# Grouped-query attention on one core: a new order of the PV matmuls, of the early loads, and of the work at the end

## The chip, the cores and the metric

One core of one Trainium2 chip. The time is the device time of one execution in microseconds (us). Times of experiments are compared with runs of the kernel before on the same chip in the same rounds. "Span" is the profiled execution from its first to its last instruction, some 1.7 us less than the device time.

## The reference, cut to what matters

```python
B, Hq, Hkv, Sq, Sk, D = 16, 32, 8, 288, 512, 128      # bf16
def reference(q, k, v):
    k = jnp.repeat(k, 4, axis=1); v = jnp.repeat(v, 4, axis=1)
    scores = jnp.einsum("bhqd,bhkd->bhqk", q, k) * D ** -0.5
    return jnp.einsum("bhqk,bhkd->bhqd", softmax(scores), v)
```

Four query heads share one key/value head, so there are 128 heads of 4 x 288 = 1152 queries (9 query tiles of 128) and 512 keys (4 key tiles of 128).

## The kernel before

Each head is cut into three chunks of 1536 score columns, 384 chunks in all. For a chunk TensorE makes the scores (S, keys on the partitions), ScalarE the exponentials, and TensorE the product with the values (PV): three query tiles, each a sum over four key tiles. A column of ones behind the 128 value columns makes the sum of the exponentials, hence 129 columns. VectorE inverts that sum and scales. Keys and values come in units of four heads, queries by head. All loads and stores are issued by the sync engine, in one fixed order. The code is abridged (`...` marks what is left out; the wrappers around the calls are dropped).

```python
    DV = D + 1                # 129
    LAG = NC + 1              # PV runs 4 chunks behind S
    NQ = 12                   # query buffers, one head each
    NO = 6                    # output buffers, one head each
    ALONE = 5 * TPC           # sums that the last check takes by themselves
    ...
        v_sb = sbuf_tensor("v_sb", [P, NSLOT, UG * NJ, DV], BF16)   # rows of 129, packed
    ...
        def op_pv(r):                      # 12 matmuls of one chunk
            waits = [("s_vc", g + 1), ("s_e", ...)]
            if 2 <= r < NS - 1:
                waits.append(("s_ev", r - 1))
            for a in range(TPC):           # query tile
                for j in range(NJ):        # key tile
                    matmul(outs(r)[:, a, :], pt_sb[..j, t..], v_sb[:, sl, gi * NJ + j, :],
                           start=(j == 0), stop=(j == NJ - 1))

        def op_ev(r):                      # VectorE: scale into an output buffer
            waits = [("s_rc", r + 1)]
            if g >= NO:                    # the buffer's last store must have landed
                waits.insert(0, ("s_o%d" % (g % NO), 16 * (g // NO)))

        # the sync engine's order: a list sorted by a time in chunks
        for u in range(1, NU):             # keys and values by unit
            t = -1.0 + u if u < NSLOT else NC * UG * (u - NSLOT + 1) + LAG
            sp.append((t, op_k(u))); sp.append((t + 0.2, op_v(u)))
        for g in range(UG, NG):            # queries by head
            sp.append((-0.9 + g / UG - 1.0 if g < NQ else NC * (g - NQ + 1) + 1.2, op_q(g)))
        for g in range(LASTG):             # output by head
            sp.append((NC * (g + 1) + LAG + 1.5, op_store(g)))
```

A kernel for any data ("general code") is built in as well. At the end a flag, made from the extremes of the sums, tells each engine whether to run it; with these inputs none does.

Of the kernel before, what the change touches and what calls it, by code (L numbers as in the profile page):

```python
# [287 lines left out]
def bass_standalone__gqa_softmax__near_ridge_kernel(  # L288
# [6 lines left out]
    B, Hq, Sq, D = q.shape  # L295
# [3 lines left out]
    NJ = Sk // P  # L299
    NT = R // P  # L300
    G = Hkv
    NG = B * G
    assert D == P and Sk % P == 0 and R % P == 0
    BANK = 512
    TPC = 3
    CH = TPC * BANK
    COLS = NJ * R
    NC = COLS // CH
# [3 lines left out]
    LAG = NC + 1  # L312
    UG = 4
    NU = NG // UG
    NSLOT = 3
    NQ = 12
    NPT = 3
    NO = 6
    NS = NG * NC
    LASTG = NG - 1  # L320
    ALONE = 5 * TPC


    q_v = q.rearrange("b h s d -> (b h s) d").rearrange("(x t) d -> x (t d)", t=NT)
# [4 lines left out]
    with ExitStack() as es:  # L329
# [29 lines left out]
        def general(eng, key, after):  # L359

            home[key] = nc.cur_bb
            eng.br(after + key)
            with nc.body("general_" + key):
                if key == "sp":
                    eng.sem_inc(sem["s_go"], 1)
                fns[key](eng)
                eng.br("done_" + key)
            nc.switch_bb(after + key)
# [20 lines left out]
        v_sb = main.enter_context(nc.sbuf_tensor("v_sb", [P, NSLOT, UG * NJ, DV], BF16))  # L389
# [4 lines left out]
        rl_sb = main.enter_context(nc.sbuf_tensor("rl_sb", [P, NG * NT], FP32))  # L394
        st_sb = main.enter_context(nc.sbuf_tensor("st_sb", [P, 2, B], FP32))
        ck_sb = main.enter_context(nc.sbuf_tensor("ck_sb", [P, 3], FP32))
        bad_sb = main.enter_context(nc.sbuf_tensor("bad_sb", [P, 2, ALONE + 1], FP32))
        one_f = main.enter_context(nc.sbuf_tensor("one_f", [P, 1], FP32))
# [6 lines left out]
        def need(eng, waits):  # L405

            left = []
            for (s, n) in waits:
                key = (id(eng), s)
                if seen.get(key, 0) < n:  # L410
                    seen[key] = n
                    left.append((sem[s], n))
            return left

        def emit(eng, waits, fn):
            waits = need(eng, waits)
            for (s, n) in waits[:-1]:
                eng.wait_ge(s, n)
            ins = fn()
            if waits:  # L420
                ins.wait_op(waits[-1][0], waits[-1][1], "sem-ge")
            return ins


        def op_k(u, gi=None):
            eng = nc.sync
            sl = u % NSLOT
            if u >= NSLOT:
                for (s, n) in need(eng, [("s_s", NC * UG * (u - NSLOT + 1))]):
                    eng.wait_ge(s, n)  # L430
            g0, g1 = (0, UG) if gi is None else (gi, gi + 1)
            eng.dma_start_transpose(  # L432
                kt_sb[:, sl, :, g0:g1].rearrange("d j g p -> d j (g p)"),
                k_v[(u * UG + g0) * P:(u * UG + g1) * P]
            ).then_inc(sem["us_k%d" % sl if gi is None else "s_k%d" % gi], 16)

        def op_v(u, gi=None):
            eng = nc.sync
            sl = u % NSLOT
            if u >= NSLOT:  # L440
                for (s, n) in need(eng, [("s_vc", UG * (u - NSLOT + 1))]):
                    eng.wait_ge(s, n)
            g0, g1 = (0, UG) if gi is None else (gi, gi + 1)
            eng.dma_start(
                vd_sb[:, sl, g0:g1], v_v[:, u * UG + g0:u * UG + g1]
            ).then_inc(sem["us_v%d" % sl if gi is None else "s_v%d" % gi], 16)

        def op_q(g):
            eng = nc.sync
            if g >= NQ:  # L450
                for (s, n) in need(eng, [("s_s", NC * (g - NQ + 1))]):
                    eng.wait_ge(s, n)
            eng.dma_start_transpose(qt_sb[:, g % NQ], q_v[g * P:(g + 1) * P]).then_inc(sem["s_q%d" % (g % NQ)], 16)
# [49 lines left out]
        def outs(r):  # L503

            if r == NS - 1:
                return ps_s[:, (NS - 2) % 2].rearrange("p (a e) -> p a e", e=BANK)[:, :, 0:DV]
            return ps_o[:, r % 2, 0:TPC * DV].rearrange("p (a e) -> p a e", e=DV)

        def op_pv(r):
            eng = nc.tensor  # L510
            g = r // NC
            sl, gi = (g // UG) % NSLOT, g % UG
            waits = [("s_vc", g + 1), ("s_e", r + 1 if g == LASTG else NC * (g + 1))]
            if 2 <= r < NS - 1:
                waits.append(("s_ev", r - 1))
            for a in range(TPC):
                t = TPC * (r % NC) + a
                for j in range(NJ):
                    ins = emit(eng, waits if a == 0 and j == 0 else [], lambda: eng.matmul(  # L519
                        outs(r)[:, a, :], pt_sb[:, g % NPT, j * R + t * P:j * R + (t + 1) * P],  # L520
                        v_sb[:, sl, gi * NJ + j, :], start=(j == 0), stop=(j == NJ - 1)))
            ins.then_inc(sem["s_pv"], 1)


# [53 lines left out]
        def op_stat(b):  # L578
            eng = nc.vector
            w = G * NT  # L580
            a, e = b * w, (b + 1) * w - (ALONE if b == B - 1 else 0)
            emit(eng, [("s_rc", e // TPC)], lambda: eng.tensor_reduce(  # L582
                st_sb[:, 0, b:b + 1], rl_sb[:, a:e], AX.X, ALU.max))
            eng.tensor_reduce(st_sb[:, 1, b:b + 1], rl_sb[:, a:e], AX.X, ALU.min).then_inc(sem["s_stat"], 1)  # L584

        def op_over(hi, lo, x0, x1, wait, n):

            eng = nc.vector
            emit(eng, [wait], lambda: eng.tensor_scalar(  # L589
                out=bad_sb[:, 0, x0:x1], in0=hi, scalar1=SUM_MAX, scalar2=None, op0=ALU.is_gt)  # L590
            ).then_inc(sem["s_stat"], 1)
            emit(eng, [("s_stat", n)], lambda: eng.scalar_tensor_tensor(  # L592
                out=bad_sb[:, 1, x0:x1], in0=lo, scalar=1.0 / SUM_MAX, in1=bad_sb[:, 0, x0:x1],
                op0=ALU.is_lt, op1=ALU.add)).then_inc(sem["s_bad"], 1)
# [2 lines left out]
        first = [lambda: op_k(0, 0), lambda: op_q(0), lambda: op_k(0, 1), lambda: op_q(1), lambda: op_v(0, 0)]  # L597
        first += [lambda: op_k(0, 2), lambda: op_q(2), lambda: op_v(0, 1)]
        first += [lambda: op_k(0, 3), lambda: op_q(3), lambda: op_v(0, 2), lambda: op_v(0, 3)]
        sp = []  # L600
        for u in range(1, NU):
            t = -1.0 + u if u < NSLOT else NC * UG * (u - NSLOT + 1) + LAG
            sp.append((t, lambda u=u: op_k(u)))
            sp.append((t + 0.2, lambda u=u: op_v(u)))
        for g in range(UG, NG):
            sp.append((-0.9 + g / UG - 1.0 if g < NQ else NC * (g - NQ + 1) + 1.2, lambda g=g: op_q(g)))
        for g in range(LASTG):
            sp.append((NC * (g + 1) + LAG + 1.5, lambda g=g: op_store(g)))
        for i in range(NC):
# [13 lines left out]
        def _(eng):  # L623
            for n in range(NS + LAG):
# [6 lines left out]
            emit(eng, [("s_ev", NS - 1), ("s_bad", 2)], lambda: eng.matmul(  # L631
                ps_o[0:1, NS % 2, 0:ALONE + 1], one_f[:], bad_sb[:, 1, :], start=True, stop=True)
            ).then_inc(sem["s_bad"], 1)
            choose(eng, "pe", behind=True)

        @block.scalar
        def _(eng):
            emit(eng, [("s_one", 1)], lambda: eng.activation(dum[:, 1:2], dum[:, 0:1], ACTF.Exp))  # L638
            for n in range(NS):
                op_exp(n)  # L640
            op_ev_last()
            general(eng, "act", "end_")
            choose(eng, "act")

        @block.gpsimd
# [7 lines left out]
        @block.vector  # L653
        def _(eng):
            eng.memset(dum[:], 0.0).then_inc(sem["s_one"], 1)  # L655
            eng.memset(one_f[:], 1.0)
            general(eng, "dve", "main_")
            per_b = G * NC
            for r in range(NS):
                op_rc(r)  # L660
                if r == NS - 1:
                    last = rl_sb[:, NG * NT - ALONE:NG * NT]
                    op_over(last, last, 0, ALONE, ("s_rc", NS), B + 3)
                op_ev(r)
                if r % per_b == per_b - 1 and r < NS - 1:
                    op_stat(r // per_b)
                if r == NS - 1 - ALONE // TPC:
                    op_stat(B - 1)
                    emit(eng, [("s_stat", B)], lambda: eng.tensor_reduce(  # L669
                        ck_sb[:, 0:1], st_sb[:, 0, :], AX.X, ALU.max))  # L670
                    eng.tensor_reduce(ck_sb[:, 1:2], st_sb[:, 1, :], AX.X, ALU.min).then_inc(sem["s_stat"], 1)  # L671
                    op_over(ck_sb[:, 0:1], ck_sb[:, 1:2], ALONE, ALONE + 1, ("s_stat", B + 1), B + 2)
            with nc.allow_low_precision(reason="a count of at most 2048"):
                emit(eng, [("s_bad", 3)], lambda: eng.tensor_reduce(  # L674
                    flag_i[:], ps_o[0:1, NS % 2, 0:ALONE + 1], AX.X, ALU.add)).then_inc(sem["s_flag"], 1)
            choose(eng, "dve")
# [30 lines left out]
```

## Time and profile before

| | before |
|---|---|
| time, median of 3 runs | 540.84 us (540.35 to 541.56) |
| span, mean TensorE clock | 539.4 us, 0.996 |
| first exponential starts | 8.18 us |
| last exponential ends | 533.16 us |
| from there to the end | 6.22 us |

Names in the lines of the profile: PE is TensorE and PEld its weight loads, ACT is ScalarE, DVE is VectorE, SPq is the sync engine issuing a load or store. `kt_sb`, `qt_sb` and `vd_sb` are the buffers into which keys, queries and values are loaded, `v_sb` the values as PV reads them, `ps_s` the scores, `pt_sb` their exponentials, `ps_o` the PV sums, `o_sb` the output buffers. L541 is line 541 of the kernel.

Two engines are busy 97% of the span, TensorE and ScalarE. From the page, the busy tenths in 40 slices of the span and the clock that TensorE was granted:

```profile
PE   4799999999999999999999999999999999999997
...
ACT  5889999999999999999999999999999999999995
...
PEclk9989999999999999999999999999999999999999
```

Only the first three slices (13.5 us each) and the last one have room in them. The single 8 of the clock row is a time at half clock, at 27 to 30 us, after the one stall.

### The profile page before, as it was taken

How to read it: one execution, taken by the hardware profiler on the slowest of the kernel's cores; microseconds unless marked ns; L12 is line 12 of the kernel's file. 1: busy time of each engine (PE TensorE's matmuls, PEld its weight loads, DVE VectorE, ACT ScalarE, POOL GpSimd, SP SyncE). 2: the span in 40 equal slices, each digit the busy share in tenths (PEclk: the TensorE clock that was granted, in tenths of full speed). 3: DMA queues.
4: the chain of work that ended last, by engine and by line, in shares of the span. 5: the costliest groups of instructions: out<-in, count | busy, mean ns of one | idle time of the engine just before them, and what ended most of it. 6: DMA issues, size and time to landing. Idle time of an engine off the chain costs nothing.

```text
span 539.4 us, 14538 instructions
## 1 busy us (share of the span) xinstructions
PE 524.0 (97%) x6152; PEld 411.2 (76%) x6152; DVE 288.5 (53%) x809; ACT 522.1 (97%) x387; POOL 73.8 (14%) x133
## 2 busy tenths in 40 slices
PE   4799999999999999999999999999999999999997
PEld 1577777777777777777777777777777777777776
DVE  0445555555555555555555555555555555555555
ACT  5889999999999999999999999999999999999995
POOL 1021211100111101111101111101111101111000
PEclk9989999999999999999999999999999999999999
DMA  6999999999899988899998999989899988995212
GB/s 133 178 216 246 281 247 292 260 203 190 219 212 228 207 209 219 192 215 232 205 183 220 219 215 233 211 186 199 224 220 225 219 182 216 204 224 154 87 67 92
DMA packets 253944, 110.08 MB, mean 204 GB/s; under 512 B 220848, under 2 KB 237616, under 8 KB 253872
## 3 DMA queue, kind: packets, MB, share of 16 engines
q1 hardware_dynamic: 253872, 109.08, 90.2%
q8 instruction: 50, 0.82, 0.6%
q14 instruction: 22, 0.18, 0.1%
HBM read 16.78 MB, written 37.75 MB: 101 GB/s over the span
## 4 chain that ended last, share of the span: by engine, by line
PE 94%; ACT 3%; DVE 1%; DMA 1%; issue 1%; SPq 0%
PE ps_o L519 49%; PE ps_s L499 45%; ACT pt_sb L537 3%; DMA qt_sb<-in_q_dram 1%; DVE o_sb L565 0%; SPq L432 0%; DVE rl_sb L554 0%; DVE bad_sb L589 0%; DVE bad_sb L592 0%; DVE ck_sb L669 0%; DVE st_sb L584 0%; DVE flag_i L674 0%; DVE st_sb L582 0%; DVE ck_sb L671 0%
## 5 line engine op out<-in xcount | busy, mean ns | idle before, releaser
L537 ACT ACTIVATE pt_sb<-ps_s 128x1536 bf16<-128x1536 f32 x384 | 520.2, 1452 | 10.6 <-PE ps_s L499 10.6
L519 PEld LDWEIGHTS ps_o<-v_sb,pt_sb 128*128 128x128 bf16 x4596 | 300.2, 98 | 55.0 <-DVE o_sb L565 0.6
L519 PE MATMUL ps_o<-v_sb,pt_sb 128*128 128x129 bf16 x4596 | 332.6, 221 | 0.4 <-DVE o_sb L565 0.4
L499 PE MATMUL ps_s<-qt_sb,kt_sb 128*128 128x512 bf16 (+3 forms) x1542 | 313.8, 326 | 11.6 <-DMA qt_sb<-in_q_dram 6.7
L565 DVE TENSOR_TENSOR o_sb<-ps_o,rl_sb 128x384 bf16<-128x384 f32 x383 | 213.6, 558 | 13.5 <-DVE rl_sb L554 0.3
L554 DVE RECIPROCAL rl_sb<-ps_o 128x3 f32<-128x3 f32 x383 | 69.3, 181 | 233.9 <-PE ps_o L519 233.9
L499 PEld LDWEIGHTS ps_s<-qt_sb,kt_sb 128*128 128x128 bf16 x1542 | 130.2, 98 | 69.5 <-DMA qt_sb<-in_q_dram 6.7
L547 POOL COPY v_sb<-vd_sb 128x512 bf16<-128x512 bf16 x128 | 73.3, 616 | 421.3 <-DMA vd_sb<-in_v_dram 392.5
L584 DVE TENSOR_REDUCE st_sb<-rl_sb 128x1 f32<-128x72 f32 (+1 forms) x16 | 3.5, 217 | 0.0
L582 DVE TENSOR_REDUCE st_sb<-rl_sb 128x1 f32<-128x72 f32 (+1 forms) x16 | 3.5, 217 | 0.0
L573 ACT ACTIVATE o_sb<-ps_s,rl_sb 128x128 bf16<-128x128 f32 x1 | 0.4, 368 | 2.9 <-DVE rl_sb L554 2.9
L638 ACT ACT_TABLE_LOAD x1 | 1.3, 1283 | 0.8 <-PEq L692 0.8
L631 PE MATMUL ps_o<-bad_sb,one_f 128*1 128x16 f32 x2 | 0.2, 176 | 0.7 <-DVE bad_sb L592 0.7
L519 PE MATMUL ps_s<-v_sb,pt_sb 128*128 128x129 bf16 x12 | 0.9, 221 | 0.0
L631 PEld LDWEIGHTS ps_o<-bad_sb,one_f 128*1 128x1 f32 x2 | 0.1, 80 | 0.9 <-DVE bad_sb L592 0.9
L519 PEld LDWEIGHTS ps_s<-v_sb,pt_sb 128*128 128x128 bf16 x12 | 0.7, 98 | 0.0
L655 DVE MEMSET dum<- 128x2 f32 x1 | 0.1, 60 | 0.9 <-PEq L692 0.9
L565 DVE TENSOR_TENSOR o_sb<-ps_s,rl_sb 128x256 bf16<-128x256 f32 x1 | 0.4, 418 | 0.0
L647 POOL MEMSET v_sb<- 128x48 bf16 x1 | 0.3, 311 | 0.3 <-POOLq L692 0.3
L638 ACT ACTIVATE dum<-dum 128x1 f32<-128x1 f32 x1 | 0.2, 203 | 0.0
L592 DVE SCALAR_TENSOR_TENSOR bad_sb<-rl_sb,bad_sb 128x15 f32<-128x15 f32 x1 | 0.2, 175 | 0.0
L589 DVE TENSOR_SCALAR bad_sb<-rl_sb 128x15 f32<-128x15 f32 x1 | 0.2, 174 | 0.0
(11 smaller groups left out, 1.4 us busy)
## 6 DMA issues: line engine op xcount, KB each, us to landing
out_dram<-o_sb SPq DMA_DIRECT2D x127, 288.0 KB, 3.4
vd_sb<-in_v_dram SPq DMA_DIRECT2D x31, 512.0 KB, 5.1
qt_sb<-in_q_dram SPq DMA_TRANSPOSE x128, 4.6
kt_sb<-in_k_dram SPq DMA_TRANSPOSE x35, 4.7
vd_sb<-in_v_dram SPq DMA_DIRECT2D x4, 128.0 KB, 2.9
out_dram<-o_sb SPq DMA_DIRECT2D x3, 96.0 KB, 1.8
```

What stands on the lines that cost most here:

```text
L499: ins = emit(eng, waits if x == 0 else [], lambda: eng.matmul(ps_s[:, n % 2, c:c + w], kt_sb[:, sl, j, gi, :], qg[:, r0:r0 + w], start=Tru ...
L519: ins = emit(eng, waits if a == 0 and j == 0 else [], lambda: eng.matmul(outs(r)[:, a, :], pt_sb[:, g % NPT, j * R + t * P:j * R + (t + 1) ...
L537: emit(eng, waits, lambda: eng.activation(dst, src, ACTF.Exp, scale=scale)).then_inc(sem["s_e"], 1)
L547: emit(eng, waits, lambda: eng.tensor_copy(v_sb[:, sl, gi * NJ:(gi + 1) * NJ, 0:D], vd_sb[:, sl, gi].rearrange("p (j d) -> p j d", d=D))). ...
L554: emit(eng, [("s_pv", r + 1)], lambda: eng.reciprocal(rl_sb[:, TPC * r:TPC * (r + 1)].unsqueeze(2), outs(r)[:, :, D:DV])).then_inc(sem["s_ ...
L565: emit(eng, waits, lambda: eng.tensor_tensor(out=o_sb[:, g % NO, t0:t0 + n, :], in0=outs(r)[:, 0:n, 0:D], in1=rl_sb[:, TPC * r:TPC * r + n ...
L573: emit(eng, [("s_o%d" % (LASTG % NO), 16 * (LASTG // NO)), ("s_rc", NS)], lambda: eng.activation(o_sb[:, LASTG % NO, NT - 1, :], outs(NS - ...
L582: emit(eng, [("s_rc", e // TPC)], lambda: eng.tensor_reduce(st_sb[:, 0, b:b + 1], rl_sb[:, a:e], AX.X, ALU.max))
L584: eng.tensor_reduce(st_sb[:, 1, b:b + 1], rl_sb[:, a:e], AX.X, ALU.min).then_inc(sem["s_stat"], 1)
L631: emit(eng, [("s_ev", NS - 1), ("s_bad", 2)], lambda: eng.matmul(ps_o[0:1, NS % 2, 0:ALONE + 1], one_f[:], bad_sb[:, 1, :], start=True, st ...
L638: emit(eng, [("s_one", 1)], lambda: eng.activation(dum[:, 1:2], dum[:, 0:1], ACTF.Exp))
L647: eng.memset(v_sb[:, :, :, D:DV], 1.0)
```

## The change

Its parts: the 12 PV matmuls of a chunk go by key tile, with the three query tiles inside; the loads of the second and third unit go out in the order in which they are needed (and the keys of every later unit go out 3.5 chunks earlier than before); ScalarE jumps over the general code at the top instead of at the end; the checks for the flag are spread over three chunks and the last one comes after the last division. The core of the diff:

```diff
-    ALONE = 5 * TPC
+    ALONE = 8 * TPC
...
-            for a in range(TPC):
-                t = TPC * (r % NC) + a
-                for j in range(NJ):
+            alone = r == NS - 1
+            for j in range(NJ):
+                for a in range(TPC):
+                    t = TPC * (r % NC) + a
                     ins = emit(eng, waits if a == 0 and j == 0 else [], lambda: eng.matmul(
...
-                        v_sb[:, sl, gi * NJ + j, :], start=(j == 0), stop=(j == NJ - 1)))
+                        v_sb[:, sl, gi * NJ + j, :], start=(j == 0 and (a == 0 or alone)), stop=(j == NJ - 1),
+                        skip_group_check=True))
...
-            t = -1.0 + u if u < NSLOT else NC * UG * (u - NSLOT + 1) + LAG
-            sp.append((t, lambda u=u: op_k(u)))
-            sp.append((t + 0.2, lambda u=u: op_v(u)))
+            t = NC * UG * (u - NSLOT + 1) if u >= NSLOT else -2 * NC * UG + u
+            sp.append((t + 0.5, lambda u=u: op_k(u)))
+            sp.append((t + (LAG if u >= NSLOT else 0.65), lambda u=u: op_v(u)))
         for g in range(UG, NG):
-            sp.append((-0.9 + g / UG - 1.0 if g < NQ else NC * (g - NQ + 1) + 1.2, lambda g=g: op_q(g)))
+            t = NC * (g - NQ + 1) + 1.2 if g >= NQ else -2 * NC * UG + g // UG + 0.51 + 0.1 * (g % UG)
+            sp.append((t, lambda g=g: op_q(g)))
...
+            general(eng, "act", "main_")          # ScalarE, ahead of its 384 exponentials
...
-            general(eng, "act", "end_")
...
+            op_over(last, last, 0, ALONE, ("s_rc", NS), B + 3)   # VectorE, after the last division
```

More of the change, by code (lines that the diff above doesn't have):

```diff
@@ L658, in _ @@
             per_b = G * NC
+            w0 = NS - 1 - ALONE // TPC
+            last = rl_sb[:, NG * NT - ALONE:NG * NT]
             for r in range(NS):
                 op_rc(r)
-                if r == NS - 1:
-                    last = rl_sb[:, NG * NT - ALONE:NG * NT]
-                    op_over(last, last, 0, ALONE, ("s_rc", NS), B + 3)
                 op_ev(r)
@@ L666, in _ @@
                     op_stat(r // per_b)
-                if r == NS - 1 - ALONE // TPC:
+                if r == w0:
                     op_stat(B - 1)
+                if r == w0 + 1:
                     emit(eng, [("s_stat", B)], lambda: eng.tensor_reduce(
@@ L671, in _ @@
                     eng.tensor_reduce(ck_sb[:, 1:2], st_sb[:, 1, :], AX.X, ALU.min).then_inc(sem["s_stat"], 1)
+                if r == w0 + 2:
                     op_over(ck_sb[:, 0:1], ck_sb[:, 1:2], ALONE, ALONE + 1, ("s_stat", B + 1), B + 2)
+            op_over(last, last, 0, ALONE, ("s_rc", NS), B + 3)
             with nc.allow_low_precision(reason="a count of at most 2048"):
```

## The prediction

> **What bounds the kernel now.** I read the page first, then the waits, then the timeline of ScalarE over the whole span and of all engines around the one stall and the end, and last the starts of single instructions in the trace. The kernel works through 384 chunks (128 heads by 3): TensorE makes 1536 columns of scores (S), ScalarE takes their exponential, TensorE multiplies the probabilities of an earlier chunk by the values (PV, 12 matmuls), VectorE divides. The page's first part and its costliest groups:
>
> ```profile
> PE 524.0 (97%) x6152; PEld 411.2 (76%) x6152; DVE 288.5 (53%) x809; ACT 522.1 (97%) x387; POOL 73.8 (14%) x133
> ...
> L537 ACT ACTIVATE pt_sb<-ps_s 128x1536 bf16<-128x1536 f32 x384 | 520.2, 1452 | 10.6 <-PE ps_s L499 10.6
> L519 PEld LDWEIGHTS ps_o<-v_sb,pt_sb 128*128 128x128 bf16 x4596 | 300.2, 98 | 55.0 <-DVE o_sb L565 0.6
> L519 PE MATMUL ps_o<-v_sb,pt_sb 128*128 128x129 bf16 x4596 | 332.6, 221 | 0.4 <-DVE o_sb L565 0.4
> ```
>
> Two engines stand at 97%, so the question is which of them sets the pace. ScalarE alone, over the span:
>
> ```profile
> 8.18 16.22 ACT L537 ACTIVATE pt_sb<-ps_s 128x1536 bf16<-128x1536 f32 x12 [5.88 <-PE ps_s L499]
> 28.46 1.45 ACT L537 ACTIVATE pt_sb<-ps_s 128x1536 bf16<-128x1536 f32 x1 [4.06 <-PE ps_s L499]
> 30.62 502.54 ACT L537 ACTIVATE pt_sb<-ps_s 128x1536 bf16<-128x1536 f32 x371 [0.71 <-PE ps_s L499]
> ```
>
> Columns are start, length, group, count, and the idle time before. One exponential lasts 1.45 us, so the first stretch runs at (16.22 - 1.45) / 11 = 1.343 us per chunk and the last at (502.54 - 1.45) / 370 = 1.354 us. In the first stretch the score matmuls wait for ScalarE ("idle before <-ACT"), so 1.343 us is ScalarE's own rate. After the stall it is slower by 11 ns per chunk. There TensorE is busy without a gap (500.00 of the 500 us from 30 to 530), and its own chunk is that long: S starts at 300.62 and PV at 301.27 (0.65 us), and the PV before ran from 299.92 to 300.62 (0.70 us), together 1.35. So **TensorE sets the pace by a hair, and ScalarE is 11 ns behind it**. The chain that ended last agrees: PE 94%, ACT 3%.
>
> The stall between the two stretches:
>
> ```profile
> 14.36 7.66 SPq L453 DMA_TRANSPOSE qt_sb<-in_q_dram  x4
> 22.05 2.15 SPq L432 DMA_TRANSPOSE kt_sb<-in_k_dram  x1
> ...
> 26.99 1.44 PE L499 MATMUL ps_s<-qt_sb,kt_sb 128*128 128x512 bf16 x4 [3.63 <-issue]
> ```
>
> The keys of the second unit (heads 4 to 7) are issued at 22.05 behind four query loads, of which three were not needed yet; they land near 27. From start to start, the two exponentials around it come 5.64 and 2.16 us after their predecessors, against 1.35: (5.64 - 1.33) + (2.16 - 1.35) = **5.1 us lost**. The second, smaller part is because TensorE came back at half clock (single matmuls of 512 columns are 428 ns apart near 27 us, 215 later).
>
> The end: the last exponential is over at 533.16, the span at 539.4, so 6.2 us of tail.
>
> **What the Trainium skill says.** "TensorE: Matmul & The Clock Gate", section "Wait — 56ns, not 53.3ns?", gives N / 2.4 GHz + about 2.5 ns from one warm matmul to the next. The trace agrees for S: medians of 215, 162, 109 and 56 ns at 512, 384, 256 and 128 columns. For PV (129 columns) the same sum gives 56.3 ns, and the medians by key tile are 57, 61, 59, 59 for the first query tile and 56, 61, 59, 59 for the next: the matmul that opens a sum runs at the formula, the three that add to the sum just written take about 3.7 ns more. 12 come to 705.5 ns where 12 x 56 = 672. No page I read explains this. The same page, "What you observe" and the states after it, has the clock at half after about one idle window of 3.4 us; the trace shows that after the stall. "PSUM — Partial Sum Buffer", section "The four PSUM rules", says that the flag that opens a sum clears the marks of its whole 2 KiB bank, and that a later first matmul without the flag overwrites where the mark is clear. That is what the new start flags rest on, so results should stay right; the trace of before can't show it. "ScalarE: Activation LUTs", section "What ACT_TABLE_LOAD costs", gives 186 ns + 0.833 ns per column, with 93 ns overlap: 1466 and 1373 ns for 1536 columns. The trace has 1450 and 1343; I use the trace.
>
> **The change part by part.**
>
> 1. PV by key tile. The same 12 matmuls and 12 weight loads per chunk; only the order changes, so that two matmuls adding to the same columns have two others between them, and only the first of the bank carries the start flag. If the 3.7 ns come from adding to what was written one matmul ago, they go: PV 672 ns, TensorE's chunk 1354 - 33 = 1321 ns, below ScalarE's 1343. Then ScalarE sets the pace and only the 11 ns are won, not the 33: 371 x 0.0113 = **4.2 us**. That ScalarE can hold 1.343 beside PV is shown: from 12.8 to 23 us PV ran too.
>
> 2. Loads of the second unit. The keys now go out first, where the first query load stood, at about 14.4; the fourth head's queries next. Keys took 4.9 us from issue to landing, queries 4.6 (median on the page). From 14.36 to 26.99 the queue brought four query loads (0.295 MB each) and the keys (0.524 MB), 1.70 MB in 12.6 us, 135 GB/s; keys and one query load are 0.82 MB, 6.1 us, so about 20.5 us, against 23.1 when the next scores are due. The rest (two more query loads, values, then the third unit) adds up to 3.05 MB at 37 us for a need at 39.3. So the stall goes: **5.1 us**. The half clock goes with it. Later units have queries 12 heads ahead (about 49 us) against landings of at most 7.7 us; that order changes nothing.
>
> 3. ScalarE passes the general code at the top. At the end its load of the flag starts only at 538.57, though the flag is ready at 536.86: its branch at 536.03 skips a large block. But the sync engine, waiting for the last store until 538.57, finishes at the same time (539.17 against 539.15). So alone: **about 0**. At the top the branch is hidden in the wait until 8.18.
>
> 4. Flag checks spread. They sit between two divisions at 531.8 to 532.7 and hold the evacuation that the PV at 533.47 waits for ("idle 0.39 <-DVE o_sb"): about 0.3 us. The last check moves behind the last division, so the last store goes out 0.3 us earlier (536.31 back to 536.01), while the flag comes about 0.4 us later and becomes the end. Together with PV being further ahead if part 1 works: **0.3 to 0.6 us**.
>
> Sum if all works: the last exponential ends at 8.18 + 1.45 + 383 x 1.343 = 524.0 against 533.16, 9.2 us (parts 1 and 2), plus 0.5: 9.7, that is 531.1 us.
>
> **The rivals.**
>
> - The 3.7 ns belong to adding as such (a fixed cost of each adding matmul), not to the distance. For it: at half clock the extra disappears (107 to 111 ns against 107.5), as the formula's 2.5 ns does too, which suits a fixed cost. Then TensorE stays at 1.354; only the stall goes, plus TensorE's lead of some 0.4 us, which it had at 23 us and then eats up at 11 ns a chunk: 5.1 + 0.4 + 0.3 = 5.8, **535.0 us**. If it belongs to matmuls without the start flag, 11 of 12 have it: 6 ns a chunk more, about 2 us, **537 us**. Against both: the opening matmul being exactly at the formula in the middle of a stream fits a wait for the previous sum as well, and that the extra is gone where the distance is 107 ns fits it too.
> - The stall stays in part, because DMA is busy already (share 0.92 from 30 to 530 us, and near 1 around the stall) and the keys land late or a later load is pushed out: up to 2 us back, **533 us**.
> - A gain over 2% (below 530.0) needs something beyond ScalarE's 384 x 1.343 = 515.7 us of work: the 8.2 us at the start are untouched, and the tail would have to lose 1.6 us. Unlikely.
>
> **Range and chances.** I give the full gain 0.63, full gain with some stall left 0.07, unchanged TensorE 0.2, slower TensorE 0.1. The middle is near 531.5; I put 531.6, and 530.4 to 535.6 holds the first three. Faster by over 2% 0.08, within 0.91, slower 0.01.
>
> **What would show it.** ScalarE in one unbroken stretch of 384 from about 8.2 us, at 1.343; score matmuls waiting for ScalarE throughout; PV starts 56 ns apart for all 12. Keys of the second unit issued near 14.4 and no TensorE wait there. Clock 1.00 from 23 to 30 us. ScalarE's wait for the flag ending with the other engines'. Wrong if PV stays near 705 ns, if a wait for loads reappears at 23 to 45 us, or if ScalarE is slower than 1.343 in a long stretch.

## The result

| | before | after |
|---|---|---|
| time, median of 4 runs | 541.2 us (540.35 to 541.76) | 537.9 us (536.35 to 538.7) |
| span, mean clock | 539.4 us, 0.996 | 537.0 us, 0.994 |
| first exponential starts | 8.18 | 8.16 |
| last exponential ends | 533.16 | 531.57 |
| from there to the end | 6.22 | 5.41 |

The ratio is 0.9937 with a 95% interval of 0.991 to 0.9964. A ratio here is the mean time of one kernel's fast runs over that of the other's of the same rounds, so it is not quite the ratio of the medians. The change gained 0.6%; I had predicted 531.6 us, and the time is outside the range of 530.4 to 535.6. The output is correct, here and in every run of the new PV order. That bears out what the prediction took from the Trainium skill, "PSUM — Partial Sum Buffer", section "The four PSUM rules": three sums stood open in one bank, with one start flag.

ScalarE after, over the whole span (start, length, group, count, idle time before):

```profile
8.15 33.69 ACT L541 ACTIVATE pt_sb<-ps_s 128x1536 bf16<-128x1536 f32 x25 [5.85 <-PE ps_s L499]
48.05 1.45 ACT L541 ACTIVATE pt_sb<-ps_s 128x1536 bf16<-128x1536 f32 x1 [6.21 <-PE ps_s L499]
50.55 481.02 ACT L541 ACTIVATE pt_sb<-ps_s 128x1536 bf16<-128x1536 f32 x358 [1.05 <-PE ps_s L499]
```

The pace is (33.69 - 1.45) / 24 = 1.343 us before the stall and (481.02 - 1.45) / 357 = 1.343 after it: the pace is ScalarE's own now, as predicted. The pace is the same in all runs below whose PV takes 683 to 694 ns, so it isn't TensorE's. The stall at 23 us is gone, as predicted. But there is a stall at 42 us that was not there, and it is longer. From end to end, the two exponentials around a stall took 5.51 + 2.16 us before, 7.66 + 2.50 after. Less two ordinary chunks that is 5.0 us lost before and 7.5 us after. The half clock, which the prediction saw go with the stall, came back with the new one: PEclk is 0.50 from 26.6 to 30.0 us before and from 43.5 to 50.3 us after, twice as long. The profiled run is also the slowest of its four (538.7 us), so the 7.5 is at the high end; the run with the loads alone, below, lost 5.5 us in the same place with 3.4 us at half clock. What VectorE and TensorE waited for:

```profile
DVE o_sb L569 <- DMA out_dram<-o_sb: 6.4, 1, 6.4
PEld ps_o L522 <- DVE o_sb L569: 5.9, 2, 5.5
PE ps_o L522 <- DVE o_sb L569: 5.4, 2, 5.2
```

Each line has the engine that waits, what it waits for, total time, times, and the longest. VectorE waited once for a *store*, and TensorE waited for VectorE. The sync engine's record has the rest of it:

```profile
14.79 2.69 SPq L432 DMA_TRANSPOSE kt_sb<-in_k_dram  x1
17.53 4.14 SPq L453 DMA_TRANSPOSE qt_sb<-in_q_dram  x2
21.71 0.59 SPq L444 DMA_DIRECT2D vd_sb<-in_v_dram  x1
22.35 3.77 SPq L453 DMA_TRANSPOSE qt_sb<-in_q_dram  x2
26.17 2.15 SPq L432 DMA_TRANSPOSE kt_sb<-in_k_dram  x1
28.35 3.97 SPq L453 DMA_TRANSPOSE qt_sb<-in_q_dram  x2
32.37 0.58 SPq L444 DMA_DIRECT2D vd_sb<-in_v_dram  x1
32.99 7.59 SPq L453 DMA_TRANSPOSE qt_sb<-in_q_dram  x4
40.62 1.24 SPq L467 DMA_DIRECT2D out_dram<-o_sb  x1
```

The first line is the keys of the second unit, at 14.8 us instead of 22.1: that repair works. The last line is the first output store, at 40.62 us. By the trace, head 0 was complete at 17.4 us; its store stood in the issue order behind 14 loads, among them the queries of heads 8 to 13. VectorE around that time:

```profile
38.07 0.18 DVE L558 RECIPROCAL rl_sb<-ps_o 128x3 f32<-128x3 f32 x1 [0.57 <-PE ps_o L522]
44.63 0.56 DVE L569 TENSOR_TENSOR o_sb<-ps_o,rl_sb 128x384 bf16<-128x384 f32 x1 [6.38 <-DMA out_dram<-o_sb]
```

At 38.3 us head 6 is ready to be scaled into its buffer. With six buffers, that is the buffer of head 0, whose store has not even been issued. It lands about 4 us after 40.62, and VectorE goes on at 44.63. The first store before, in the sync engine's record:

```profile
40.01 0.58 SPq L467 DMA_DIRECT2D out_dram<-o_sb  x1
```

And VectorE before, at the same place, head 6:

```profile
43.52 0.18 DVE L554 RECIPROCAL rl_sb<-ps_o 128x3 f32<-128x3 f32 x1 [0.58 <-PE ps_o L519]
43.74 0.56 DVE L565 TENSOR_TENSOR o_sb<-ps_o,rl_sb 128x384 bf16<-128x384 f32 x1
```

The store was just as late before (40.01). But the load stall had delayed head 6 to 43.74 us, 3.7 us after the issue, while stores land after 3.4 us (median on the page). The store wait was there all along, hidden behind the load stall: by the trace that store landed at 43.22, half a microsecond before head 6 needed its buffer.

The account of the two profiled spans: pace, 370 chunks x 11 ns, -4.0 us; stall, 7.5 for 5.0, +2.5 us; the part after the last exponential, -0.8 us; sum -2.3, measured 537.0 - 539.4 = -2.4 us.

One more line needs care, ScalarE's group on the page after:

```profile
L541 ACT ACTIVATE pt_sb<-ps_s 128x1536 bf16<-128x1536 f32 x384 | 516.2, 1723 | 13.1 <-PE ps_s L499 13.1
```

The mean length of one exponential rose from 1452 to 1723 ns while the pace went down to 1343. These records overlap, so the pace has to be read from the stretches, not from the mean length.

The end after, from the timeline of all engines:

```profile
533.61 0.18 DVE L558 RECIPROCAL rl_sb<-ps_s 128x3 f32<-128x3 f32 x1
533.82 0.42 DVE L569 TENSOR_TENSOR o_sb<-ps_s,rl_sb 128x256 bf16<-128x256 f32 x1
...
534.16 0.17 DVE L593 TENSOR_SCALAR bad_sb<-rl_sb 128x24 f32<-128x24 f32 x1
534.36 0.18 DVE L596 SCALAR_TENSOR_TENSOR bad_sb<-rl_sb,bad_sb 128x24 f32<-128x24 f32 x1
```

The last division now comes ahead of the last check. ScalarE loads the flag 3.5 us after the last exponential, with all others, where it loaded it 5.4 us after it before; VectorE's way through the flag ends last.

### The profile page after: what moved, and what is told of

It reads as the page before. It is cut to its first block, busy times and chain, and to the rows that moved or that the text cites. A ratio compares the mean times of both kernels' runs of the same rounds, so it can differ in the third digit from the quotient of the medians.

```text
span 537.0 us, 14438 instructions
## 1 busy us (share of the span) xinstructions
PE 514.8 (96%) x6052; PEld 405.9 (76%) x6152; DVE 288.3 (54%) x809; ACT 518.0 (96%) x387; POOL 73.7 (14%) x133
## 4 chain that ended last, share of the span: by engine, by line
PE 93%; DMA 2%; issue 1%; SPq 1%; ACT 1%; DVE 1%; POOL 0%; DVEq 0%; POOLq 0%
PE ps_o L522 49%; PE ps_s L499 44%; DMA vd_sb<-in_v_dram 1%; DMA qt_sb<-in_q_dram 1%; ACT pt_sb L541 1%; DMA out_dram<-o_sb 1%; DVE o_sb L569 0%; SPq L432 0%; SPq L453 0%; POOL v_sb L551 0%; DVE rl_sb L558 0%; SPq L467 0%; PE ps_o L637 0%; DVE bad_sb L596 0%; DVE flag_i L682 0%
## 5 line engine op out<-in xcount | busy, mean ns | idle before, releaser
L541 ACT ACTIVATE pt_sb<-ps_s 128x1536 bf16<-128x1536 f32 x384 | 516.2, 1723 | 13.1 <-PE ps_s L499 13.1
L522 PEld LDWEIGHTS ps_o<-v_sb,pt_sb 128*128 128x128 bf16 x4596 | 295.8, 98 | 60.6 <-DVE o_sb L569 5.9
L522 PE MATMUL ps_o<-v_sb,pt_sb 128*128 128x129 bf16 x4596 | 327.4, 221 | 6.7 <-DVE o_sb L569 5.4
L499 PE MATMUL ps_s<-qt_sb,kt_sb 128*128 128x512 bf16 (+3 forms) x1442 | 298.7, 324 | 12.2 <-DMA qt_sb<-in_q_dram 6.7
L499 PEld LDWEIGHTS ps_s<-qt_sb,kt_sb 128*128 128x128 bf16 x1542 | 117.4, 98 | 67.0 <-DMA qt_sb<-in_q_dram 6.6
```

What stands on the lines that cost most here:

```text
L499: ins = emit(eng, waits if x == 0 else [], lambda: eng.matmul(ps_s[:, n % 2, c:c + w], kt_sb[:, sl, j, gi, :], qg[:, r0:r0 + w], start=Tru ...
L522: ins = emit(eng, waits if a == 0 and j == 0 else [], lambda: eng.matmul(outs(r)[:, a, :], pt_sb[:, g % NPT, j * R + t * P:j * R + (t + 1) ...
L541: emit(eng, waits, lambda: eng.activation(dst, src, ACTF.Exp, scale=scale)).then_inc(sem["s_e"], 1)
```

## The experiments

Two questions: does the store wait explain the missing 6 us, and why did PV get faster? On the second, the steps from one PV matmul to the next did not come out as I had predicted. They are read from the start times of single matmuls in the trace, medians over chunks 30 to 370, in the order of issue (medians, because some matmul records are missing from the traces); sums are from the first PV start to the next S start:

| kernel | steps in ns | sum |
|---|---|---|
| before | 57 61 59 59, 56 61 59 59, 56 60 59 59 | 705 |
| after | 57 57 57, 61 56 56, 61 56 56, 60 56 57 | 688 |

I had predicted 12 steps of 56. Before, the long ones are key tiles 1 to 3 of each query tile. After, they are key tiles 1 to 3 of the first query tile only, although the other two add just as much. So adding to the sum just written is not what costs, and what else changes at those places is the tile of values.

### Only the new PV order

```diff
 the kernel before, with the new loop over j and a and the new start flags; loads and end as before
```

> The kernel before with only the new order of the PV matmuls. Theory (the new order takes the pace from TensorE, the new load order exchanged one stall for another): ScalarE at 1.343 us per chunk, the load stall near 23 us still there (about 5 us, perhaps 1 us of store wait after it), 536.5 to 537.5 us, as fast as the whole change. Rival (the new load order is worth its 5 us and something else lost them): clearly slower than the whole change, 539 us or more.

Measured: 536.6 us (534.5 to 538.9), ratio 0.9916 (0.9871 to 0.996). ScalarE:

```profile
8.41 16.27 ACT L539 ACTIVATE pt_sb<-ps_s 128x1536 bf16<-128x1536 f32 x12 [6.12 <-PE ps_s L499]
27.54 1.45 ACT L539 ACTIVATE pt_sb<-ps_s 128x1536 bf16<-128x1536 f32 x1 [2.86 <-PE ps_s L499]
...
31.86 497.14 ACT L539 ACTIVATE pt_sb<-ps_s 128x1536 bf16<-128x1536 f32 x370 [0.63 <-PE ps_s L499]
```

The old stall, and then 1.343 us per chunk. This one part does as well as the whole change. The 1 us of store wait that was held possible is not there.

### Only the new load order

```diff
 the kernel before, with the new times of op_k, op_v and op_q; PV and end as before
```

> The kernel before with only the new order of the loads. Theory: ScalarE stays at 1.354 us per chunk, no wait near 23 us, but VectorE waits near 39 us for the first output store, 5 to 7 us, ScalarE idle as long; 541 to 543 us, no gain. Rival (the store wait comes from the faster PV, not from the loads): no wait near 39 us, 535.0 to 536 us.

Measured: 542.2 us (541.3 to 542.8), ratio 1.0019 (0.9989 to 1.0048). ScalarE:

```profile
8.37 33.69 ACT L537 ACTIVATE pt_sb<-ps_s 128x1536 bf16<-128x1536 f32 x25 [6.07 <-PE ps_s L499]
47.51 486.35 ACT L537 ACTIVATE pt_sb<-ps_s 128x1536 bf16<-128x1536 f32 x359 [5.46 <-PE ps_s L499]
```

From the waits of the same run, total, times and longest:

```profile
DVE o_sb L565 <- DMA out_dram<-o_sb: 5.4, 1, 5.4
```

The store wait comes with the load order alone, at the old pace of 1.354. It replaces the old stall, and the run as a whole gains nothing.

### The changed kernel with more output buffers

```diff
-    NO = 6
+    NO = 12
```

> The changed kernel with 12 output buffers in place of 6, nothing else. Theory (the wait is for an output buffer whose store was issued late): ScalarE in one stretch of 384 at 1.343, span about 529.5, time 530.4 to 531.5. Rival (the DMA queue is simply short of throughput in the first 50 us): the store wait goes but a wait for queries, keys or values follows it, 533 to 538 us.

Measured: 531.4 us (531.15 to 531.5), ratio 0.9819 (0.9793 to 0.9845). ScalarE:

```profile
8.26 2.79 ACT L541 ACTIVATE pt_sb<-ps_s 128x1536 bf16<-128x1536 f32 x2 [5.96 <-PE ps_s L499]
11.27 513.26 ACT L541 ACTIVATE pt_sb<-ps_s 128x1536 bf16<-128x1536 f32 x382 [0.21 <-PE ps_s L499]
```

The first store still goes out at 39.7 us, but nothing waits for it, and no wait for loads takes its place, so the rival, a queue short of throughput, is out. The last exponential ends at 524.5 us; the prediction's sum had 524.0. So the store wait is the whole of what was missing.

### The changed kernel with fewer query buffers

```diff
-    NQ = 12
+    NQ = 8
```

> The changed kernel with 8 query buffers in place of 12, so that four query loads (heads 8 to 11) no longer stand ahead of the first store. Theory (stores late because loads run too far ahead): first store issued near 33 us in place of 40.6, no store wait, 530.4 to 531.5 us. Rival (queries need the depth of 12): waits for queries, slower than the changed kernel.

Measured: 531.7 us (531.3 to 531.9), ratio 0.9823 (0.9797 to 0.9849). The sync engine's first store:

```profile
31.82 0.58 SPq L467 DMA_DIRECT2D out_dram<-o_sb  x1
```

Four query loads fewer ahead of it (those of heads 10 to 13; the text above names the wrong heads) bring the first store 8.8 us forward, in time for head 6. The time is 0.2 us above the range expected. Taking buffers away does what doubling the output buffers does. So the buffers are enough; what makes the store late is its place in the issue order.

### Value rows on other boundaries

```diff
-        v_sb = ... [P, NSLOT, UG * NJ, DV]        # the kernel before
+        v_sb = ... [P, NSLOT, UG * NJ, 160]       # PV reads columns 0 to DV, as before
```

> The kernel before, with only the rows of the values in the on-chip buffer 160 elements apart in place of 129, so that every key tile starts at a multiple of 64 bytes. In the changed kernel the long matmuls are only those that go to another key tile's values (the first query tile of key tiles 1 to 3), so adding alone does not make them long. Theory A (the odd start of the values costs 3 to 5 ns when a matmul turns to them): PV near 672 ns in the old order too, ScalarE at 1.343, load stall as before, 536 to 537.5 us. Theory B (turning to other values, or to a far probability tile, costs it wherever they start): PV stays 705, 540.5 to 541.5 us.

Measured: 536.7 us (534.75 to 538.6), ratio 0.9931 (0.9891 to 0.997); all steps 57 ns but the last, sum 683 (672 was expected); pace 1.343. With its old order of matmuls, the kernel before gets what the new order got.

In the profiled execution the load stall was short: ScalarE was idle for 2.69 us in it, where the kernel before has 4.06. Head 6 then came earlier, and the store wait that the kernel before hides comes out, with loads in the old order (the longest, 1.0 us, is head 6 waiting for the first store):

```profile
DVE o_sb L565 <- DMA out_dram<-o_sb: 1.6, 2, 1.0
```

Two more widths, one look each, so that their sums and paces count and not their times: kernels with a stall spread by 1.3 to 4.4 us from run to run in this record, those without (12 output or 8 query buffers) by 0.6 us at most.

> The kernel before with value rows 130 elements apart (260 bytes: key tiles start at multiples of 4 bytes). If an odd 2-byte start is what costs, PV is 683 to 690 ns as with 160; if a wider boundary is needed, the long steps stay at some of the key tiles (59 to 61 ns) and PV is between 683 and 705.

> The same with rows 132 apart (264 bytes: multiples of 8 bytes). If 8 bytes suffice, PV 683 ns with even steps of 57; if it takes 64 bytes, steps of 59 to 61 stay and PV is nearer 705.

Measured: with 130 the steps stay long at key tiles 1, 2 and 3 (sum 704, pace 1.351, 540.2 us). With 132 they are long at key tiles 1 and 3 and short at 2 (57 61 56 59, 56 59 56 59, 56 60 56 59; sum 694, pace 1.343, 537.4 us). Of the expectations, "an odd 2-byte start" misses: 130 removes it and changes next to nothing. With 132 neither branch holds: the steps are not even, and the sum lies midway between 683 and 705. Nor is it the boundary of the start as such, because with 129 every other head has its key tile 0 at 8 bytes off a multiple of 16 (counted from the start of the buffer), and that step is as short there as in the rest (56.6 to 56.7 ns on average in all). What fits these: the value rows are packed, and a matmul is long where its values start in the same 16 bytes in which those of the matmul ahead of it ended. With 132 elements (264 bytes), key tile 0 ends at byte 257 and tile 1 starts at 264, the same 16; tile 1 ends at 521 and tile 2 starts at 528, another 16; tile 2 ends at 785 and tile 3 starts at 792, the same 16. That is the pattern seen.

### Nothing adds

```diff
-                        ... start=(j == 0), stop=(j == NJ - 1)))
+                        ... start=True, stop=True, skip_group_check=True))
```

> The kernel before with the start flag on every PV matmul, so that nothing adds (wrong result on purpose). Theory of the prediction (adding to what was just written costs the time): PV 672 ns in 12 even steps of 56. Rivals A and B (the operands cost it): PV stays at 705 ns with the same 56, 61, 59, 59.

Measured: the result is wrong; the steps are 57 61 59 59, 56 61 59 59, 56 60 59 59 and the sum 705, the same as before. The explanation in my prediction is refuted, and with it the rival that each adding matmul has a fixed cost.

### Another order of the key tiles

If a neighbour's start is what costs, it is enough not to take neighbours one after another.

```diff
-                for j in range(NJ):                      # the kernel before
+                for j in (0, 2, 1, 3):                   # start at 0, stop at 3
```

> The kernel before with the key tiles of each sum taken in the order 0, 2, 1, 3, value rows 129 apart as they were. Theory C (a PV matmul is long where its values start in the same 16 bytes in which those of the matmul ahead of it ended; that fits all runs so far): no key tile follows its neighbour, so PV is 672 to 683 ns in even steps of 56 to 57, ScalarE at 1.343, load stall as before, 535 to 538 us. Theory A (the start itself must be a multiple of 16 bytes or more): long steps stay at key tiles 2, 1 and 3, PV 705, 540.5 to 541.5 us.

> The same with the order 3, 2, 1, 0. Theory C, where only a start right behind the last end counts: PV even, 672 to 683 ns. If neighbours cost in either direction: long steps stay, PV near 705 ns.

Measured: order 0, 2, 1, 3: 536.7 us (536.0 to 537.3), ratio 0.9899 (0.9874 to 0.9923), sum 684, pace 1.343. Order 3, 2, 1, 0, one look: sum 684, pace 1.343, 535.2 us. The sums are within 1 ns of what was expected (672 to 683) and of the padded rows, and refute the theory that the start itself must lie on a boundary. But the single steps are less even than expected. In the first order the matmul of key tile 2, which follows tile 0, takes 59 ns; in the second that of tile 3, where it follows tile 0, takes 59 as well. The rule of the 16 bytes has no long step there, and why they are long is not shown. The short steps after them make up for most of it (57 59 56 56 is 228 ns, against 235 to 236 before). So the rule accounts for the sums, not for every step: rows packed at 129 cost a chunk next to nothing as long as no tile starts where the last one ended.

### Only the two small parts

```diff
 the kernel before, with general(eng, "act", "main_") at the top and the checks spread as in the change
```

> The kernel before with only the two small parts: ScalarE passes the general code at the top, flag checks spread. Theory: last exponential to end of span 6.2 us before, 5.5 to 5.9 here, all else the same; time 0.3 to 0.7 us less than before, inside the noise (540 to 541.5 us).

Measured: 540.65 us, ratio 1.000 (0.9956 to 1.0044), no difference to be seen in the time. In the trace, 5.78 us from the last exponential to the end, where 6.22 were before: 0.4 us.

### Old PV order, padded rows, new loads, fewer query buffers

```diff
 the kernel before, with value rows of 160, the new times of op_k, op_v and op_q, and NQ = 8
```

> The kernel before with value rows 160 apart, the new order of the loads and 8 query buffers, but the old order of the PV matmuls and the old end. Theory (the starts of the value rows set the PV time, and ScalarE's 384 x 1.343 is then the floor): as fast as the changed kernel with 8 query buffers, 531.3 to 532.5 us. Rival (the new PV order gives something besides): 533 us or more.

Measured: 531.5 us (531.3 to 531.9), ratio 0.9816 (0.98 to 0.9832). ScalarE:

```profile
8.10 515.94 ACT L537 ACTIVATE pt_sb<-ps_s 128x1536 bf16<-128x1536 f32 x384 [5.80 <-PE ps_s L499]
```

One unbroken stretch, (515.94 - 1.45) / 383 = 1.343 us. It reaches the changed kernel with 8 query buffers (531.7) without the new PV order. These two and the one with 12 output buffers beat both kernels by 6 us or more (compared across rounds). They all end at the same limit: 384 exponentials at 1.343 us, plus 8 us at the start and 5 to 6 at the end.

## Why the prediction was right or wrong

**Who sets the pace: right.** TensorE's chunk was 11 ns longer than ScalarE's, and any relief of PV by more than that hands the pace to ScalarE at 1.343. "4.2 us" was worth 4.0.

**Why PV gets shorter: wrong, without harm to the sum.** The step said "If the 3.7 ns come from adding to what was written one matmul ago, they go: PV 672 ns". PV went to 688, and the run in which nothing adds has 705. The extra time goes with reading values right behind the last ones: the new order does that 3 times a chunk, the old one 9 times. That the pace passed to ScalarE all the same is partly luck. Had PV needed to fall below 688 to clear ScalarE's pace, the sum would have failed as well: 688 leaves TensorE only some 6 ns of room (S takes 1354 - 705 = 649, and 688 + 649 = 1337 against 1343), not the 22 predicted.

**The loads: the step that failed.** It said "So the stall goes: 5.1 us", after adding up only the loads that had to arrive. The old stall went; the time did not. A store of the first head shares the issue order with those loads, and it leaves near 40 us in every run with 12 query buffers (39.3 to 40.8). The 5 us at 23 us were hiding a wait of 5 to 7 us at 38 us, and the load order alone measures 1.0019. In place of -5.1 the term is +2.5 in the profiled run of the changed kernel. With 12 output buffers or 8 query buffers in the changed kernel, neither stall is left. The rival "the stall stays in part" had the size wrong (up to 2 us) and the place wrong: it looked for late loads, and none was late. I never asked when the first store would be due.

**The small parts: right in kind, small in size.** 0.3 to 0.6 us foreseen, 0.4 alone, 0.8 with the faster PV, which is above the range.

**The range** left out one of the prediction's four cases, a slower TensorE at 537 us. The measured time is near that figure by chance: the pace was 1.343, not slower. None of the four had a wait that the old stall had covered.

## What to carry to other kernels

Before a stall is counted as gain, go to the next thing that each engine needs after it, and see how long that has been ready: what was ready only just in time becomes the next stall. Loads that run far ahead of their use stand ahead of stores in the same issue order; a buffer less can be faster. Where matmul steps differ by a few nanoseconds, look at where their operands lie, and try a padded row or another order of the sum before other explanations.

## What the Trainium skill lacked or had wrong

- "SBUF — State Buffer", section "Specifications (TRN2)", says that the memory has 16-byte cachelines and that "each cross to a new line pays a penalty". The size agrees with what the runs show, but from one PV matmul to the next the effect is the other way about: one whose values start in the 16 bytes in which those of the matmul ahead ended takes 59 to 61 ns, one that starts elsewhere 56 to 58, but for a 59 in each of two orders (sums of 12: 705 with rows of 129, 704 with 130, 694 with 132, 683 with 160, 684 with 129 in another order). Why is not shown.
- "TensorE: Matmul & The Clock Gate", section "Wait — 56ns, not 53.3ns?", has one formula for the step between warm matmuls. It holds for S and for the short PV steps (56 to 57 ns at 129 columns) and misses the long ones by 3 to 5 ns. The page has nothing on where the moving operand starts.
- "ScalarE: Activation LUTs", section "What ACT_TABLE_LOAD costs", gives figures that make 1466 ns for one exponential of 1536 columns and 1373 for the pace; measured 1450 and 1343.
- No page that I read says that loads issued well ahead can hold up a store in the same issue order; here the first store left at 40.6 us with 12 query buffers and at 31.8 with 8.
